# Fused softcap attention and max-out layer on one core: another order for the first eleven quads of pairs

## The chip, the core and the metric

The kernel runs on one core of a Trainium2 chip. TensorE (PE) multiplies, ScalarE (ACT) does tanh and exp, VectorE (DVE) adds, copies and normalizes, GpSimd (POOL) issues the loads, and SyncE (SP) issues the stores, the crossbar transposes and some of the signals between engines. Each engine takes its own instructions in the order in which the program has them, and waits for others by semaphores. The metric is the device time of one execution in microseconds (us), the median of the runs shown; less is better.

## What is computed

Attention with 8 batches, 12 heads, 448 positions and 64 features a head, whose scores go through a soft cap, and then a layer whose two branches are joined by a maximum:

```python
scores = (1 / 8) * q @ k.T
scores = 30 * np.tanh(scores / 30)
attn = np.exp(scores - scores.max(-1))
attn = attn / (attn.sum(-1) + 1e-9)
out = attn @ v                      # (8, 12, 448, 64)
x = out.transpose(0, 2, 1, 3).reshape(3584, 768)
g = np.maximum(x @ w1, x @ w2)      # (3584, 1024)
result = g @ w_out                  # (3584, 768)
```

Inputs and output are float32. The kernel works in bfloat16 with float32 sums. It uses max(a, b) = b + relu(a - b): it subtracts w2 from w1 once (`wd_sb`), multiplies w2 and w_out once (`wm_sb`), and computes x @ wm + relu(x @ wd) @ w_out.

## The kernel before

**Tiles.** Two heads make a pair i (0 to 47) and two pairs a quad t (0 to 23); six pairs are a batch. Scores are computed transposed, with the keys on the partitions: three blocks of 128 keys for each pair (j = 0 to 2) and the 64 left-over keys of a whole quad together. There are two score tiles in PSUM, s0 and s1, of two banks each, and four single banks, 0 to 3, for everything else. A score tile is written by S or L, read by a tanh, and lent once a quad to the value products (VL, V), until the normalization (N) has read it.

**The order.** The whole program is a list, `ORDER`, written out by hand: a semicolon between steps, each a name and numbers. The loop at the end runs it step by step (lines 737 to 740), and each step issues its instructions to its engine. So the list fixes the order on every engine, and nothing is rescheduled. Where a step stands relative to steps of other engines matters only for which data it finds and which buffers are free. The steps:

| step | engine | what it does |
|---|---|---|
| ld0, cd, Xh, XCh | SP/ACT, ACT/DVE, PE, DVE | load, cast, transpose and copy the first pair |
| lq, lk, lv, lw1, lw2, lwo | POOL | load q, k, v, and parts of w1, w2, w_out (casting) |
| D bank n | PE | n blocks of 128 columns of warming products, four to an instruction (`keep_warm`, line 466); their result is not used |
| X i bank, XC i | PE, DVE | transpose q and k of pair i (line 453), copy to `qkT` (458) |
| W c bank, WC c | PE, DVE | transpose part c of w2 (411), copy (415) |
| OP, P c h n, PC c h | PE, DVE | n of the eight premultiplies for part c, half h of `wm_sb` (426), copy (432) |
| S i j, T i j, E i j0 j1 | PE, ACT, ACT | scores (509), tanh (514), exp (531) of pair i |
| L t, TL t, EL t | PE, ACT, ACT | the same for the left-over keys (523, 527, 534) |
| VL t, V t u j0 j1 | PE | value products of quad t (595, 601), half u |
| A, B | DVE | sums of exponentials over key blocks, from quad 3 on (543, 548) |
| Y t bank, Y1 to Y3, N t u | PE, DVE | sum over keys (561, 565, 568), inverse (573 to 579), normalize into `xT` (613, 616) |
| sub c | DVE | a piece of w1 - w2 (397) |
| O g bank, M x y n | PE | open group g; n steps of groups x and y (640) |
| ev g, eva g | DVE, ACT | evict a finished group (661 for `gT`, 697 or 695 for the output rows) |
| Hs g, H g | SP, DVE | hand group g's bank over (649) |
| cr t, st b t | SP | crossbar transpose of quad t, from quad 5 on (470); store rows (671 to 676) |

**Groups and hand-overs.** A group is one bank's accumulation of the layer: stage 1 (448 columns, x @ wd) or stage 2 (384 columns, the output). A step M x y does one product of group x on rows 0 to 63 of the array and one of group y on rows 64 to 127, side by side. Each group goes through both halves, one after the other. When it changes its half, `Group.step` lets the new half's product wait for an empty instruction that `hand_over` had put on SP (Hs) or DVE (H), and which itself waits for the last product of the old half. If the list has no hand-over for a change of halves, there is no such wait. As SP and DVE take their instructions in order, a hand-over runs only when what is ahead of it on that engine has run.

**What sets the order around the change.** Quads 0 to 4 are transposed by TensorE (X, XC) and quads from 5 on by the crossbar on SP's queue (cr); there are two `qkT` buffers and two `kqs` buffers that the loads fill. The first quads also carry the setup of the weights (W, P, sub). From about quad 6 on each quad repeats a similar pattern.

Of the kernel before, what the change touches and what calls it, by code (L numbers as in the profile page):

```python
# [9 lines left out]
ld0 q; ld0 q 1; cd q; ld0 k; ld0 k 1; ms; dm; ms0; cd k; id; lq 2 0; lk 3 0; lq 3 0; lk 2 0; lw2 3; lw2 2; D 3 24;  # L10
Xh 0 0 0; Xh 0 1; cd k 1 1; cd q 1 1; XCh 0 1; XCh 0 0; D 3 4; X 1 1; S 0 0; S 0 1; XC 1; T 0 0; T 0 1; D 0 5; D 1 8;
# [8 lines left out]
X 5 0; P 2 1 4; P 0 0 3; P 2 1 1; XC 5; PC 1 1; PC 0 0; T 3 2; T 4 0; E 3 2 3; OP 3 1 3; P 3 1 1; P 2 1 1; S 4 1;  # L20
S 4 2; Y 1 1; T 4 1; T 4 2; L 2; P 3 1 4; VL 1; TL 2; V 1 1 0 3; V 1 0 0 3; S 5 0; X 6 0; E 4 0 3; T 5 0; EL 2; Y1 1;
Y2 1; PC 2 1; Y3 1; N 1 1; N 1 0; XC 6; X 7 2; W 4 1; S 5 2; S 5 1; X 8 0; P 3 1 3; WC 4; XC 8; PC 3 1; T 5 1; T 5 2;
OP 4 0 1; P 4 0 2; OP 0 1 0; P 0 1 3; S 6 0; S 6 1; W 5 3; P 0 1 1; P 4 0 6; P 0 1 4; E 5 0 2; T 6 1; T 6 0; E 5 2 3;
XC 7; sub 2 0; WC 5; sub 4 0; PC 4 0; sub 0 0; PC 0 1; OP 5 1 3; P 5 1 4; S 6 2; L 3; Y 2 1; T 6 2; TL 3; E 6 0 3;
# [36 lines left out]
M 25 24 1; S 17 1; lk 22 1; M 25 24 2; ev 22; M 25 24 1; T 17 1; S 17 2; lq 22 0; M 25 24 1; ev 23; M 25 24 1;
# [139 lines left out]
def kernel(  # L201
# [17 lines left out]
    B, H, S, D = q.shape  # L219
# [554 lines left out]
```

## Time and profile before

| | us |
|---|---|
| median of 3 runs | 328.32 |
| lowest and highest | 327.58, 328.42 |
| the profiled execution | 328.19 |
| its span, first to last instruction | 326.4 |
| TensorE busy | 319.9 |
| ScalarE busy | 281.0 |
| VectorE busy | 240.2 |
| GpSimd busy | 161.8 |

The profile is one execution. A row of a timeline gives start, duration, engine, line, operation, the tiles written and read, shape and count; in brackets stand the idle time ahead of it and what ended that. Rows of one line that follow each other are merged. "Idle" and "busy" of TensorE come from modelled ends of pipelined matmuls, so distances between starts say more than busy time. The queue of an engine that issues a DMA has rows of its own (SPq, POOLq), whose duration is that of issuing; the landing comes later.

### The profile page before, as it was taken

Reading aid. Unit: us, or ns where it says so; the run is one execution under the profiler, and the core shown is the slowest. Engines: PE = TensorE matmul, PEld = TensorE weight load, DVE = VectorE, ACT = ScalarE, POOL = GpSimd, SP = SyncE. Lnnn points to the kernel's source line nnn. Section 1 sums busy time; section 2 is a strip of 40 time slices with the busy share of each in tenths; the row PEclk is TensorE's granted clock in tenths of the full one; section 3 lists DMA queues with packets and bytes.
Section 4 is the critical chain, followed back from the end, with each engine's and each line's share of the span. In section 5 each row is a group of like instructions: output and inputs, shape, how many; then the busy total and the mean of one; then the engine's idle time right before and its main releaser. Section 6 shows DMA issues by size and latency. Waiting matters only on the chain.

```text
span 326.4 us, 9772 instructions
## 1 busy us (share of the span) xinstructions
PE 319.9 (98%) x4138; PEld 183.6 (56%) x4138; DVE 240.2 (74%) x422; ACT 281.0 (86%) x278; POOL 161.8 (50%) x237
## 2 busy tenths in 40 slices
PE   7999999999999999999999999999999999999994
PEld 3454545545656664565565565556466555557662
DVE  3346899987897778987897788968878779773201
ACT  5999999999999999999999999999999999921120
POOL 7357583677764682665775475578538311000000
PEclk9999999999999999999999999999999999999999
DMA  8999999899999999999999999999999963013033
GB/s 181 180 201 178 273 252 115 95 141 140 189 183 109 142 189 184 97 89 181 167 181 113 202 106 189 121 166 163 184 109 90 212 157 44 2 50 98 0 98 96
DMA packets 134507, 46.28 MB, mean 142 GB/s; under 512 B 112320, under 2 KB 129472, under 8 KB 134464
## 3 DMA queue, kind: packets, MB, share of 16 engines
q0 software_dynamic: 94592, 25.02, 77.6%
q1 hardware_dynamic: 39424, 19.99, 29.9%
q8 instruction: 32, 0.52, 0.7%
q10 hardware_dynamic: 448, 0.66, 0.6%
q14 instruction: 11, 0.09, 0.1%
HBM read 47.78 MB, written 11.01 MB: 180 GB/s over the span
## 4 chain that ended last, share of the span: by engine, by line
PE 94%; DMA 2%; DVE 1%; POOL 1%; issue 0%
PE mm L640 61%; PE s L509 9%; PE s L601 9%; PE mm L426 5%; DMA w2b<-in_moe_w_dram 2%; PE s L523 2%; PE mm L568 2%; PE s L595 2%; PE mm L635 1%; POOL kqs L316 1%; PE mm L453 1%; PE mm L411 1%; PE mm L561 1%; DVE xT L616 0%; PE mm L466 0%; DVE xT L613 0%
## 5 line engine op out<-in xcount | busy, mean ns | idle before, releaser
L514 ACT ACTIVATE e<-s 128x896 bf16<-128x896 f32 x144 | 125.7, 926 | 5.5 <-PE s L509 5.0
L531 ACT ACTIVATE e<-e 128x1792 bf16<-128x1792 bf16 (+2 forms) x72 | 122.8, 1708 | 0.0
L640 PE MATMUL mm<-wo_sb,gT 64*128 64x384 bf16 x864 | 115.2, 323 | 0.0
L640 PE MATMUL mm<-wm_sb,xT 64*128 64x384 bf16 x648 | 102.1, 322 | 0.0
L640 PE MATMUL mm<-xT,wd_sb 64*128 64x448 bf16 x768 | 97.6, 349 | 0.0
L323 POOL DMA_DIRECT2D kqs<-in_k_dram x76 | 54.6, 720 | 55.1 <-DMA qkT<-kqs 50.9
L640 PEld LDWEIGHTS <-gT 64*128 64x128 bf16 x864 | 58.6, 94 | 25.6 <-issue 1.1
L640 PEld LDWEIGHTS <-wd_sb 64*128 64x128 bf16 x768 | 48.3, 94 | 27.1 <-issue 2.1
L640 PEld LDWEIGHTS <-xT 64*128 64x128 bf16 x648 | 50.1, 94 | 18.5 <-issue 0.2
L509 PE MATMUL s<-qkT 64*128 64x448 bf16 x288 | 52.5, 352 | 0.2 <-DVE xT L613 0.2
L347 POOL DMA_DIRECT2D vp<-in_v_dram x48 | 30.4, 637 | 37.4 <-PE s L509 25.4
L661 DVE TENSOR_SCALAR gT<-mm 128x448 bf16<-128x448 f32 x64 | 39.0, 618 | 8.4 <-PE mm L640 7.6
L323 POOL DMA_DIRECT2D kqs<-in_q_dram x38 | 35.0, 922 | 3.9 <-issue 1.8
L601 PE MATMUL s<-e,vp 128*32 128x448 bf16 x576 | 36.1, 354 | 0.0
L543 DVE TENSOR_TENSOR esum<-e 128x896 bf16<-128x896 bf16 x42 | 25.9, 618 | 9.1 <-ACT e L531 9.1
L616 DVE TENSOR_TENSOR xT<-s,inv 64x448 bf16<-64x448 f32 x48 | 29.8, 622 | 1.7 <-PE s L601 0.8
L543 DVE TENSOR_TENSOR esum<-esum,e 128x896 bf16<-128x896 bf16 x42 | 26.2, 624 | 5.9 <-ACT e L531 4.8
L509 PEld LDWEIGHTS <-qkT 64*128 64x128 bf16 x288 | 18.7, 94 | 20.1 <-issue 11.3
L695 ACT COPY osb<-mm 128x384 f32<-128x384 f32 x10 | 4.8, 479 | 26.9 <-PE mm L640 26.7
L697 DVE COPY osb<-mm 128x384 f32<-128x384 f32 x44 | 23.3, 554 | 6.2 <-PE mm L640 5.7
L548 DVE TENSOR_TENSOR esum<-esum,el 64x896 bf16<-64x896 bf16 x42 | 26.0, 619 | 1.2
L573 DVE STREAM_TRANSPOSE st<-mm 128x448 f32<-128x448 f32 x24 | 15.6, 649 | 12.9 <-PE mm L568 11.3
(57 smaller groups left out, 269.9 us busy)
## 6 DMA issues: line engine op xcount, KB each, us to landing
out_dram<-osb SPq DMA_DIRECT2D x54, 192.0 KB, 4.8
vp<-in_v_dram POOLq DMA_DIRECT2D x38, 160.0 KB, 3.9
kqs<-in_q_dram POOLq DMA_DIRECT2D x46, 112.0 KB, 5.3
kqs<-in_k_dram POOLq DMA_DIRECT2D x76, 56.0 KB, 3.9
osb<-in_moe_w_dram POOLq DMA_DIRECT2D x4, 512.0 KB, 6.9
w2b<-in_moe_w_dram POOLq DMA_DIRECT2D x6, 256.0 KB, 7.7
wo_sb<-in_moe_w_out_dram POOLq DMA_DIRECT2D x4, 384.0 KB, 9.9
vp<-in_v_dram POOLq DMA_DIRECT2D x10, 128.0 KB, 7.8
```

What stands on the lines that cost most here:

```text
L323: nc.gpsimd.dma_start(out=to, in_=x)
L347: nc.gpsimd.dma_start(out=to, in_=x)
L509: scored[i, j] = nc.tensor.matmul(s[:, h, :S], k_of(t, o, h, j), q_of(t, o, h)).ins
L514: nc.scalar.activation(expo[i][:, 2 * j : 2 * j + 2, :], slots[i, j][:, :, :S], AF.Tanh, scale=scale / cap)
L531: nc.scalar.activation(e, e, AF.Exp, scale=float(cap))
L543: nc.vector.tensor_add(d, e[:, 0:2, :] if j == 1 else d, e[:, 2 * j : 2 * j + 2, :])
L548: nc.vector.tensor_add(d, d, left_e[t][r, :, :])
L601: nc.tensor.matmul(vals[t][place(m, u), u, :S], w[:, m, :], expo[2 * t + o][:, 2 * j + h, :], start=False, stop=(j == NJ - 1))
L616: nc.vector.tensor_mul(x[64 - r : 128 - r], vals[t][r : r + 64, u, :S], sums[t, 3][64 - r : 128 - r])
L640: ins = nc.tensor.matmul(self.ps, w[r], x[r], start=first, stop=self.at == [self.n, self.n]).ins
L661: nc.vector.tensor_relu(gT[b // 2][:, f, cs], ps)
L697: nc.vector.tensor_copy(o[:, hs], ps)
```

## The change

The list `ORDER` is written anew up to the products of quad 10 (about the first 140 us of the span). On POOL the order is the same, load by load. On the other engines the same steps stand in another order up to quad 10, with these differences in kind: banks of many steps (W, OP, X, Y, O) change; groups 24, 26 and 29 are evicted by ScalarE (eva) instead of VectorE (ev); groups 1, 10, 12, 17, 24 and 27 get a hand-over at a change of halves where there was none, group 40 gets its second one from SP instead of DVE, and several others change between SP and DVE. Warming products are as many as before (96 blocks); six of them stand between W 3 and W 2 and others move within the first pairs. From S 23 0 on each engine's order is the old one, except for the hand-overs of group 40; the text of the list differs there as well, since steps of different engines stand otherwise among each other. The instructions of TensorE are the same in number and kind over the whole program.

In `transposes`, the condition for taking a new bank asks whether a bank is named; for the steps in both lists the outcome is the same.

The diff, cut:

```diff
-ld0 q; ld0 q 1; cd q; ld0 k; ld0 k 1; ms; dm; ms0; cd k; id; lq 2 0; lk 3 0; lq 3 0; lk 2 0; lw2 3; lw2 2; D 3 24;
...
-D 3 1; D 1 4; S 0 2; D 1 4; L 0; D 1 16; T 0 2; TL 0; E 0 0 3; D 1 12; S 1 2; S 1 0; X 3 3; X 2 0; W 3 2; W 2 1;
-T 1 0; T 1 2; lw2 1; lwo 0 0; lwo 0 1; lw2 0; lq 4 0; lk 4 0; lv 0 0; lv 0 1; XC 3; XC 2; WC 3; D 0 4; S 1 1; D 0 8;
-D 2 2; S 2 1; W 1 2; WC 2; WC 1; T 1 1; T 2 1; S 2 0; D 0 4; L 1; OP 3 0 0; P 3 0 2; OP 1 0 1; P 1 0 4; P 3 0 2;
-OP 2 0 3; P 2 0 7; P 1 0 1; P 2 0 1; P 1 0 1; P 3 0 2; P 1 0 2; PC 2 0; PC 1 0; E 1 2 3; E 1 0 2; TL 1; T 2 0; EL 0;
-S 3 0; S 2 2; P 3 0 1; W 0 2; P 3 0 1; X 4 3; T 2 2; T 3 0; VL 0; Y 0 1; V 0 0 0 3; V 0 1 0 3; S 3 1; lwo 1 0;
...
-st 0 1; M 16 14 1; Hs 15; T 14 1; cr 8; B 6 0; M 16 15 1; S 14 2; M 16 15 1; ev 14; M 16 15 1; T 14 2; O 17 2;
-M 17 15 2; H 16; M 17 15 1; B 6 1; M 17 16 2; E 13 2 3; M 17 16 1; ev 15; O 18 3; M 18 16 1; L 7; VL 6; A 6 1 2;
...
-O 26 3; M 26 24 1; T 17 2; M 26 24 1; A 8 0 1; Hs 25; S 18 0; M 26 24 1; lk 23 0; M 26 25 1; A 8 0 2; M 26 25 1;
-Hs 24 2; E 17 0 2; M 26 25 1; S 18 1; lk 23 1; M 24 25 1; Hs 26; M 24 25 4; lq 23 0; M 24 25 3; T 18 0; O 27 0;
-M 27 25 1; A 8 1 1; M 27 25 1; cr 10; M 27 25 1; M 27 26 1; ev 24; M 27 26 1; T 18 1; M 27 26 1; S 18 2; ev 25;
...
+lv 0 1; E 0 0 3; lwo 1 0; S 1 2; S 1 0; X 3 3; lwo 1 1; X 2 0; XC 3; lq 5 0; W 3 2; XC 2; T 1 0; D 3 2; lk 5 0;
+D 1 4; W 2 3; WC 3; T 1 2; lv 1 0; S 1 1; WC 2; D 2 4; lv 1 1; T 1 1; S 2 1; D 0 8; T 2 1; S 2 0; W 1 0; T 2 0; L 1;
+WC 1; TL 1; S 2 2; OP 2 0 3; P 2 0 2; T 2 2; P 2 0 1; OP 3 0 0; P 3 0 1; OP 1 0 2; P 1 0 2; P 3 0 1; E 1 2 3;
+P 3 0 2; S 3 0; P 1 0 1; EL 0; P 3 0 2; P 1 0 1; P 2 0 1; P 3 0 1; T 3 0; P 3 0 1; P 2 0 1; P 1 0 1; PC 3 0; P 1 0 1;
+P 2 0 1; E 1 0 2; P 1 0 2; P 2 0 1; W 0 1; PC 1 0; S 3 1; WC 0; X 4 0; T 3 1; Y 0 2; XC 4; lk 8 0; EL 1; lq 8 0;
...
+M 15 14 1; T 14 0; S 14 1; A 6 1 1; O 16 1; M 16 14 1; Hs 15; st 0 1; lq 18 0; M 16 14 2; M 16 15 1; T 14 1; B 6 1;
+M 16 15 1; S 14 2; lk 19 0; M 16 15 1; A 6 0 2; O 17 2; M 17 15 1; T 14 2; M 17 15 1; Hs 16; cr 8; M 17 15 1; B 6 0;
+lk 19 1; M 17 16 2; E 13 2 3; L 7; ev 15; lq 19 0; VL 6; V 6 0 0 2; TL 7; A 6 1 2; V 6 1 0 2; V 6 0 2 3; ev 14;
+st 0 2; E 14 0 3; V 6 1 2 3; Y 6 0; lv 8 0; M 17 16 1; Hs 17; Y1 6; O 18 3; M 18 16 1; S 15 0; M 18 16 1; lv 8 1;
...
+Hs 25; cr 10; M 26 24 1; Hs 24; M 26 25 1; E 17 2 3; lk 23 0; M 26 25 2; M 24 25 2; lk 23 1; S 18 1; E 17 0 2;
+M 24 25 3; lq 23 0; S 18 2; M 24 25 2; Hs 26; M 24 25 1; st 1 3; O 27 0; M 27 25 2; T 18 1; M 27 25 1; A 8 1 1;
+M 27 26 4; T 18 2; A 8 1 2; M 27 26 4; B 8 1; eva 24; L 9; VL 8; ev 25; TL 9; V 8 1 0 2; B 8 0; V 8 1 2 3; st 1 4;
...
-        if c != 1:
+        if bank is not None:
             turned["qk", i] = mm_tile(bank).bitcast(bf16)
```

More of the change, by code (lines that the diff above doesn't have):

```diff
@@ L20 @@
[L20 to L24, printed above, removed]
@@ L195 @@
[L195 to L196 removed]
+ld0 q; ld0 q 1; ld0 k; ld0 k 1; ms; dm; ms0; D 3 24; id; lq 2 0; lk 3 0; lq 3 0; lk 2 0; cd k; cd q; Xh 0 0 0; lw2 3;
+Xh 0 1; cd k 1 1; D 3 4; lw2 2; XCh 0 1; cd q 1 1; XCh 0 0; lw2 1; X 1 1; lwo 0 0; S 0 0; XC 1; S 0 1; T 0 0; D 0 5;
+lwo 0 1; D 1 8; T 0 1; D 3 1; lw2 0; D 1 4; S 0 2; lq 4 0; D 1 4; T 0 2; L 0; lk 4 0; D 1 16; TL 0; lv 0 0; D 1 12;
@@ new lines @@
+M 8 9 1; Y3 4; EL 5; M 8 9 1; Hs 10; M 8 9 1; S 11 1; M 8 9 1; N 4 0; M 8 9 1; T 11 1; M 8 9 3; N 4 1; O 11 0;
+M 11 9 3; E 11 0 2; M 11 10 5; ev 9; M 11 10 1; S 11 2; M 11 10 1; ev 8; M 11 10 2; T 11 2; lq 16 0; M 11 10 1;
+A 5 1 1; S 12 0; M 11 10 1; O 12 2; M 12 10 1; T 12 0; M 12 10 1; H 11; A 5 0 2; M 12 10 1; lv 6 3; S 12 1;
+M 12 11 1; Hs 10; cr 7; B 5 1; M 12 11 1; T 12 1; lv 6 0; M 12 11 1; M 10 11 1; S 12 2; B 5 0; M 10 11 1; lk 16 1;
+M 10 11 1; T 12 2; M 10 11 4; lk 17 0; M 10 11 1; E 11 2 3; O 13 1; M 13 11 1; ev 10; L 6; st 0 0; lk 16 0; VL 5;
@@ new lines @@
+T 29 1; lv 15 2; M 55 54 1; ev 52; S 29 2; M 55 54 1; ev 53; M 55 54 1; lv 15 3; O 56 3; M 56 54 1; T 29 2;
+M 56 54 1; Hs 55; A 14 0 1; S 30 0; M 56 54 1; lk 34 1; M 56 55 2; E 29 0 2; A 14 0 2; Hs 54; M 56 55 1; S 30 1;
+lq 34 0; M 54 55 1; Hs 56; cr 16; M 54 55 5; lk 35 0; M 54 55 2; T 30 0; O 57 1; M 57 55 1; A 14 1 1; M 57 55 1;
+lk 35 1; M 57 55 1; M 57 56 1; ev 54; T 30 1; M 57 56 2; S 30 2; st 3 3; lq 35 0; ev 55; M 57 56 2; T 30 2;
+M 57 56 1; B 14 0; M 57 56 4; B 14 1; E 29 2 3; M 57 56 1; st 3 4; O 58 2; M 58 56 2; L 15; VL 14; A 14 1 2; TL 15;
@@ new lines @@
+V 14 0 0 2; V 14 1 0 2; E 30 0 3; Y 14 0; V 14 0 2 3; V 14 1 2 3; Y1 14; S 31 0; M 58 56 1; M 58 57 1; Y2 14;
+M 58 57 1; Hs 56; M 58 57 1; Y3 14; M 56 57 2; Hs 58; M 56 57 1; lk 36 0; M 56 57 1; N 14 0; M 56 57 2; T 31 0;
+M 56 57 1; lv 16 0; M 56 57 1; N 14 1; O 59 0; M 59 57 2; EL 15; M 59 57 1; lv 16 1; M 59 58 1; S 31 1; M 59 58 2;
+lv 16 2; T 31 1; M 59 58 1; ev 56; S 31 2; M 59 58 1; ev 57; M 59 58 1; lv 16 3; M 59 58 1; T 31 2; M 59 58 1;
+A 15 0 1; S 32 0; lk 36 1; M 59 58 3; E 31 0 2; A 15 0 2; O 60 3; M 60 58 1; lq 36 0; S 32 1; Hs 59; M 60 58 2;
@@ new lines @@
+M 60 59 2; Hs 58; lk 37 0; M 60 59 1; M 58 59 2; T 32 0; Hs 60; cr 17; M 58 59 1; A 15 1 1; M 58 59 1; lk 37 1;
+M 58 59 3; T 32 1; B 15 0; M 58 59 1; lq 37 0; S 32 2; O 61 1; M 61 59 1; ev 58; M 61 59 1; T 32 2; M 61 59 1;
+M 61 60 1; B 15 1; M 61 60 2; st 3 5; E 31 2 3; O 62 2; M 62 60 1; ev 59; M 62 60 2; H 61; L 16; ev 60; VL 15; TL 16;
+st 3 6; V 15 0 0 2; A 15 1 2; V 15 1 0 2; E 32 0 3; M 62 61 1; Y 15 0; V 15 0 2 3; V 15 1 2 3; Y1 15; S 33 0;
+M 62 61 2; Y2 15; O 63 3; M 63 61 1; Y3 15; M 63 61 1; Hs 62; M 63 61 1; M 63 62 1; T 33 0; M 63 62 1; N 15 0;
@@ new lines @@
+M 81 79 1; M 81 80 1; lq 44 0; M 81 80 1; ev 78; S 39 2; S 40 0; M 81 80 1; ev 79; T 39 2; O 82 3; M 82 80 1;
+lk 45 0; M 82 80 1; Hs 81; A 19 0 1; M 82 80 1; M 82 81 1; E 39 0 2; M 82 81 1; lk 45 1; ev 80; S 40 1; M 82 81 1;
+O 83 2; M 83 81 1; A 19 0 2; M 83 81 1; lq 45 0; Hs 82; cr 21; M 83 81 1; M 83 82 2; ev 81; M 83 82 1; T 40 0;
+M 83 82 2; A 19 1 1; M 83 82 3; T 40 1; M 83 82 1; B 19 0; S 40 2; M 83 82 2; T 40 2; O 84 0; M 84 82 1; B 19 1;
+M 84 82 2; H 83; H 82; E 39 2 3; M 84 83 3; M 82 83 1; L 20; A 19 1 2; VL 19; TL 20; V 19 0 0 2; V 19 1 0 2;
@@ new lines @@
+E 40 0 3; Y 19 1; V 19 0 2 3; V 19 1 2 3; Y1 19; lk 46 0; S 41 0; M 82 83 2; Y2 19; lv 21 0; M 82 83 2; Y3 19;
+M 82 83 2; lv 21 1; M 82 83 1; O 85 1; M 85 83 1; N 19 0; M 85 83 2; T 41 0; lv 21 2; M 85 84 2; N 19 1; M 85 84 2;
+lv 21 3; EL 20; M 85 84 2; S 41 1; M 85 84 1; lk 46 1; M 85 84 1; T 41 1; M 85 84 1; ev 82; S 41 2; M 85 84 1;
+lq 46 0; ev 83; M 85 84 1; O 86 3; M 86 84 1; T 41 2; M 86 84 1; Hs 85; A 20 0 1; S 42 0; M 86 84 1; M 86 85 1;
+lk 47 0; M 86 85 1; E 41 0 2; A 20 0 2; Hs 84; M 86 85 1; S 42 1; M 84 85 1; Hs 86; lk 47 1; cr 22; M 84 85 4;
@@ new lines @@
+lq 47 0; M 84 85 3; T 42 0; O 87 2; M 87 85 1; A 20 1 1; M 87 85 2; M 87 86 1; ev 84; T 42 1; M 87 86 2; S 42 2;
+st 5 3; ev 85; M 87 86 2; T 42 2; M 87 86 1; B 20 0; M 87 86 4; B 20 1; E 41 2 3; M 87 86 1; st 5 4; O 88 0;
+M 88 86 2; L 21; VL 20; A 20 1 2; TL 21; V 20 0 0 2; V 20 1 0 2; E 42 0 3; Y 20 1; V 20 0 2 3; V 20 1 2 3; Y1 20;
+S 43 0; lv 22 0; M 88 86 1; M 88 87 1; Y2 20; M 88 87 1; Hs 86; M 88 87 1; Y3 20; lv 22 1; M 86 87 2; Hs 88;
+M 86 87 2; N 20 0; lv 22 2; M 86 87 2; T 43 0; M 86 87 2; N 20 1; lv 22 3; O 89 1; M 89 87 2; EL 21; M 89 87 1;
@@ new lines @@
+M 89 88 1; S 43 1; M 89 88 2; T 43 1; M 89 88 1; ev 86; S 43 2; M 89 88 1; ev 87; M 89 88 2; T 43 2; M 89 88 1;
+A 21 0 1; S 44 0; M 89 88 3; E 43 0 2; A 21 0 2; O 90 3; M 90 88 1; S 44 1; Hs 89; M 90 88 2; M 90 89 2; Hs 88;
+M 90 89 1; M 88 89 2; T 44 0; Hs 90; cr 23; M 88 89 1; A 21 1 1; M 88 89 4; T 44 1; B 21 0; M 88 89 1; S 44 2;
+O 91 2; M 91 89 1; ev 88; M 91 89 1; T 44 2; M 91 89 1; M 91 90 1; B 21 1; M 91 90 2; st 5 5; E 43 2 3; O 92 0;
+M 92 90 1; ev 89; M 92 90 2; H 91; L 22; ev 90; VL 21; TL 22; st 5 6; V 21 0 0 2; A 21 1 2; V 21 1 0 2; E 44 0 3;
@@ new lines @@
+M 104 102 2; Hs 103; M 104 102 1; M 104 103 2; Hs 102; M 104 103 1; M 102 103 2; Hs 104; st 6 1; M 102 103 6;
+O 105 0; M 105 103 2; eva 102; M 105 103 1; M 105 104 2; eva 103; M 105 104 1; O 106 1; M 106 104 2; Hs 105;
+M 106 104 1; M 106 105 2; ev 104; M 106 105 1; O 107 2; M 107 105 2; Hs 106; M 107 105 1; M 107 106 2; ev 105;
+M 107 106 1; O 108 3; M 108 106 2; Hs 107; st 6 2; M 108 106 1; M 108 107 2; ev 106; M 108 107 1; O 109 0;
+M 109 107 2; H 108; M 109 107 1; M 109 108 2; ev 107; M 109 108 1; O 110 1; M 110 108 2; Hs 109; M 110 108 1;
@@ new lines @@
+M 110 109 2; ev 108; M 110 109 1; O 111 2; M 111 109 2; Hs 110; M 111 109 1; M 111 110 2; ev 109; M 111 110 1;
+O 112 3; M 112 110 2; Hs 111; M 112 110 1; M 112 111 2; ev 110; M 112 111 1; O 113 0; M 113 111 2; Hs 112;
+M 113 111 1; M 113 112 2; ev 111; M 113 112 9; O 114 1; M 114 112 2; Hs 113; M 114 112 1; M 114 113 2; Hs 112;
+M 114 113 1; M 112 113 2; Hs 114; M 112 113 6; O 115 2; M 115 113 2; eva 112; M 115 113 1; M 115 114 2; eva 113;
+M 115 114 3; st 7 3; M 115 114 6; O 116 3; M 116 114 2; Hs 115; M 116 114 1; M 116 115 2; Hs 114; M 116 115 1;
@@ L197 @@
+M 114 115 2; Hs 116; M 114 115 6; O 117 0; M 117 115 2; eva 114; M 117 115 1; M 117 116 2; eva 115; M 117 116 3;
+st 7 4; M 117 116 6; M -1 116 2; Hs 117; M -1 116 1; M -1 117 2; Hs 116; M -1 117 1; M 116 117 8; M -1 117 2;
+eva 116; M -1 117 1; O 118 1; M 118 118 1; eva 117; M 118 118 4; st 7 5; M 118 118 9; O 119 2; M 119 119 2; ev 118;
+M 119 119 12; ev 119; st 7 6;
 """
```

292 lines of the change are left out of this document (122 added, 170 removed).

## Prediction

> **What bounds the kernel now.** I read the page first: the span, the engine totals and the chain that ended last.
>
> ```profile
> span 326.4 us, 9772 instructions
> PE 319.9 (98%) x4138; PEld 183.6 (56%) x4138; DVE 240.2 (74%) x422; ACT 281.0 (86%) x278; POOL 161.8 (50%) x237
> ...
> PE 94%; DMA 2%; DVE 1%; POOL 1%; issue 0%
> ```
>
> TensorE is busy for 98% of the span, and 94% of the chain is its own. The change rewrites the stretch from about 12 to 138 us, so I read that stretch by stages (columns: stretch, its length, then PE, PEld, DVE, ACT and POOL busy, clock, DMA share, GB/s), and then who TensorE waited for.
>
> ```profile
> 12.00:20.00 8.00, 7.59 (x78) 4.26 (x73) 3.31 (x6) 7.84 (x9) 3.48 (x6) 1.00 1.27 199
> 20.00:62.00 42.00, 41.82 (x598) 21.54 (x598) 36.33 (x61) 42.00 (x41) 25.11 (x39) 1.00 1.22 195
> 62.00:108.00 46.00, 46.00 (x602) 26.89 (x600) 39.15 (x70) 44.72 (x45) 31.73 (x45) 1.00 1.36 143
> 108.00:138.00 30.00, 30.00 (x399) 17.11 (x399) 24.93 (x44) 29.11 (x30) 17.69 (x25) 1.00 1.34 160
> ```
> ```profile
> PE mm L411 <- DMA w2b<-in_moe_w_dram: 0.4, 1, 0.4
> PE s L509 <- DVE xT L613: 0.2, 1, 0.2
> ```
>
> The granted clock is 1.00 throughout. Two engines are full: TensorE everywhere, ScalarE from 20 to 62 us. The waits list shows 0.6 us of TensorE waits in the stretch, but a matmul's end is modelled, so a short wait can hide behind a "busy" one. I therefore count by starts.
>
> **The ledger.** The rows below (TensorE's timeline: start, duration, line, operation, count) give intervals from one start to the next.
>
> ```profile
> 12.15 0.62 PE L411 MATMUL mm<-ident,w2b 128*128 128x128 bf16 x8
> 13.18 0.62 PE L411 MATMUL mm<-ident,w2b 128*128 128x128 bf16 x8 [0.41 <-DMA w2b<-in_moe_w_dram]
> ...
> 20.35 0.55 PE L509 MATMUL s<-qkT 64*128 64x448 bf16 x4
> 20.84 0.34 PE L426 MATMUL mm<-wo_sb,w2T 128*128 128x384 bf16 x1
> ...
> 23.35 1.31 PE L601 MATMUL s<-e,vp 128*32 128x448 bf16 x24
> 24.59 0.36 PE L509 MATMUL s<-qkT 64*128 64x448 bf16 x2
> ...
> 34.58 1.07 PE L453 MATMUL mm<-ident,kqs 64*64 64x64 bf16 x56
> 35.58 0.62 PE L411 MATMUL mm<-ident,w2b 128*128 128x128 bf16 x8
> 36.36 0.55 PE L509 MATMUL s<-qkT 64*128 64x448 bf16 x4 [0.16 <-DVE xT L613]
> ...
> 58.51 2.81 PE L640 MATMUL mm<-xT,wd_sb 64*128 64x448 bf16 x28
> 61.16 0.35 PE L509 MATMUL s<-qkT 64*128 64x448 bf16 x2
> ...
> 138.63 0.36 PE L509 MATMUL s<-qkT 64*128 64x448 bf16 x2
> ```
>
> Fourteen pairs of 448 columns take 61.16 - 58.51 = 2.65, or 0.189 each; by columns a 384-wide pair or single is 0.163. Two score pairs take 20.84 - 20.35 = 0.49, which is two of 0.189 and 0.1 for the change of the array's mode; six groups of four value products in 24.59 - 23.35 = 1.24 leave the same 0.1. From the first W at 12.15 to S 23 0 at 138.63, both orders issue the same products: 171 pairs of 448 columns in M, 181 of 384, 96 P, 64 S, 66 V groups, 6 W (0.457), 6 X (0.464), 22 L and VL (0.20), 8 short Y (0.189), 3 long Y (0.77), 18 warming blocks of 128 columns (0.053); the small kinds are read from their own rows in the same way, as two X from 34.58 to 35.58. That is 116.75 us. Both orders also change mode 73 times, 7.3 us. The work is 124.05 us in either; before it took 126.48. So 2.42 us of waits and lags is all that the reordering can remove, whatever else it does. Behind S 23 0 every engine runs its old order, and ahead of W 3 nothing changes.
>
> **What goes.** The second W started 1.03 behind the first instead of 0.457: 0.57. S 5 2 started 0.78 behind its W instead of 0.557: 0.22. The other 1.63 is spread over small lags that no row names.
>
> **What stays or comes.** For the new order I walk TensorE along the ledger and ask at each S, V, Y and M whether its input is there.
>
> *A, 0.25.* The new order puts six warming blocks (0.32) between the two W, so the second could start at 12.15 + 0.457 + 0.32 = 12.93. Its weights still land where the load queue put them, just ahead of 13.18.
>
> *B, 0.42.* S 2 2 moves ahead of the premultiplies. It writes the score tile that T 2 0 reads.
>
> ```profile
> 12.48 3.73 ACT L514 ACTIVATE e<-s 128x896 bf16<-128x896 f32 x4
> ...
> 28.23 1.72 ACT L514 ACTIVATE e<-s 128x896 bf16<-128x896 f32 x2
> 29.83 0.96 ACT L531 ACTIVATE e<-e 128x896 bf16<-128x896 bf16 x1
> ```
>
> A tanh follows the one before after 0.80 and ends 0.93 behind its start. S 1 1 is at 13.18 + 0.557 = 13.74, its tanh at 14.14 (the product takes 0.36), T 2 1 at 14.94, T 2 0 at 15.74, over at 16.67. S 1 1, four warming blocks, S 2 1, eight blocks, S 2 0, W 1 and L 1 take 2.56 on the ledger, so S 2 2 is due at 16.30 and waits. In return ScalarE's pause among those four tanhs (3.73 against 3 x 0.80 + 0.93) shrinks, and it runs 0.5 ahead up to 47 us. The places where TensorE then meets it (S 3 2, Y 1, S 5 2) come out free, so the 0.22 is gone. VectorE's chain behind N 2 1 has the same work and starts about 0.6 earlier, so N 3 1 ends in time for S 9 2.
>
> *Loads, 0.* The load queue keeps its order. lk 8 waits for X 4, which the ledger puts 0.2 later.
>
> ```profile
> 22.42 0.55 POOL L316 DMA_DIRECT2D kqs<-in_k_dram x1 [0.80 <-PE mm L453]
> ...
> 24.62 0.53 POOL L316 DMA_DIRECT2D kqs<-in_q_dram x1 [1.10 <-DMA wo_sb<-in_moe_w_out_dram]
> ```
>
> The queue stops for 1.10 us two loads later for a landing that does not depend on X 4; this covers the 0.2. Without the cover, 0.2 would reach X 7.
>
> *Evictions, 0.* Groups 24, 26 and 29 are evicted by ScalarE: three of about 0.48.
>
> ```profile
> L695 ACT COPY osb<-mm 128x384 f32<-128x384 f32 x10 | 4.8, 479 | 26.9 <-PE mm L640 26.7
> ```
>
> That is 1.4 us; ScalarE's idle time in 62 to 138 us was 1.28 + 0.89 = 2.2 (the stages above). Behind them stand TL 9, T 19 1 and E 19 2, for which V 9 and S 19 wait; without that cover it is 1.4.
>
> *C, 0.3, and D, 1.25: SyncE's queue.* The crossbar transposes (cr), the stores and the hand-overs Hs share it.
>
> ```profile
> L470 SPq DMA_TRANSPOSE qkT<-kqs x19: 1301/1598/2663, 55.1 to 262.2; - x19
> ...
> DMA to landing us min/median/max: 4.2/6.3/9.5
> ```
> ```profile
> 55.50 0.75 PE L640 MATMUL mm<-xT,wd_sb 64*128 64x448 bf16 x6
> ```
> ```profile
> 55.06 1.58 SPq L470 DMA_TRANSPOSE qkT<-kqs  x1
> ```
> ```profile
> L649 SPq EVENT_SEMAPHORE  x1: 17/17/17, 56.7 to 56.7; - x1
> ```
> ```profile
> 87.02 2.19 SPq L470 DMA_TRANSPOSE qkT<-kqs  x1
> 89.27 1.26 SPq L676 DMA_DIRECT2D out_dram<-osb  x2
> ```
> ```profile
> DMA to landing us min/median/max: 7.8/7.8/7.8
> ```
> ```profile
> 95.82 0.54 PE L509 MATMUL s<-qkT 64*128 64x448 bf16 x4
> ```
> ```profile
> L649 SPq EVENT_SEMAPHORE  x3: 17/17/17, 107.6 to 108.8; - x3
> ```
> ```profile
> 109.11 1.59 SPq L470 DMA_TRANSPOSE qkT<-kqs  x1
> ```
>
> Issuing a transpose holds the queue for 1.30 to 2.66 us. The hand-over of group 3 shows that nothing passes: its products were over by about 56.1 (two of the three pairs at 55.50), yet it ran at 56.7, when the issue that began at 55.06 had ended at 56.64. There it cost nothing; group 3 went on at 58.5. The new order has, on this queue, Hs 25, cr 10, Hs 24, with only six pairs of products between the last M 25 24 and the M 24 25 that needs Hs 24. Counted from the start of that last M 25 24: it ends after 0.32, Hs 25 runs, the transpose's issue begins 0.33 later (108.8 to 109.11) and lasts 1.60, Hs 24 and TensorE's answer take about 0.1: 2.39 in all. M 24 25 is due after 0.163 + 6 x 0.163 = 1.14. TensorE stands for 1.25, from 0.95 to 2.3 with the shortest and the longest issue. Queued behind M 24 25 is everything: TensorE has one queue, and S 18 1, for which ScalarE waits, comes next. The Trainium skill (DMA: Bandwidth & Descriptors, Issuing engines are not separate DMA queues) says that starting a DMA takes an issuing sequencer a time that is usually small relative to the DMA itself. By that rule D would be about 0 and the time 327.5; this trace differs, with 1.6 of 6.3 us. C is the same thing milder: cr 8 now comes behind Hs 16, whose products end at 86.7, so its issue starts near 87.05, and the store behind it holds the queue until about 90.5. Hs 17 is needed at 90.4 (0.2 late), and S 16 0, now due at 94.6 instead of 96.0 (the second pair of the 95.82 row), meets a landing at 87.05 + 7.8 = 94.85 (the transfer begun at 87.02 has the landing row of 7.8; all nineteen took 4.2 to 9.5): 0.1, with what Hs 17 moved it. Bounds 0 and 0.5.
>
> *E, 0.8.* Lags with no name: 0 if the new order has none, 1.6 if all recur. The kinds and number of mode changes are the same, so I take half.
>
> Sum: 0.25 + 0.42 + 0.3 + 1.25 + 0.8 = 3.02, against 2.42: 0.6 longer. The profiled execution took 328.19, with 326.4 of span and 1.8 around it (median of the runs 328.32). Forecast 328.8; its own range, from the bounds of C, D and E, is 327.4 to 330.8.
>
> **Rivals.** *Nothing is held* (faster). If the transfer is handed to the queue early enough, or TensorE does not need Hs 24 so soon, D is 0; with half of E as well, 2.42 - 0.25 - 0.42 - 0.3 - 0.4 = 1.05 is won: 327.1. For it: ScalarE and VectorE meet TensorE in time everywhere I looked. Against it: the row at 56.7.
>
> *The eighth transpose lands late* (slower). S 16 0 has lost the 1.2 us that it had behind cr 8's landing (94.8 against 96.0). If that transfer takes the longest seen, 9.5 instead of 7.8, TensorE stands 1.7 more: 330.5. It decides from a landing after 95.4, and each further us is a us. Against it: the median is 6.3.
>
> *The early gain does not come* (about the same or slower). VectorE is at 36.33 of 42 us in 20 to 62; if its order makes N 1, N 3 or Y 3 late by what ScalarE gained, another 0.5: 329.3.
>
> **How the numbers follow.** Forecast 0.62, nothing held 0.14, late landing 0.20, no early gain 0.04. About 0.3%, 1 us, is what a measurement of this kernel can tell from no change: 327.3 to 329.3 around the median. The forecast's spread puts 0.03 below, 0.38 within and 0.21 above this. Faster is 0.03 + 0.14 = 0.17; same 0.38 + 0.03 = 0.41; slower 0.21 + 0.20 + 0.01 = 0.42. The range 327.2 to 330.4 leaves out most of the first rival and the end of the second.
>
> **What would show it.** A gap of about 1.2 us on TensorE in front of the first M 24 25 near 108 us, with Hs 24 directly behind a transpose's issue; the second W's wait shrunk to 0.25 and a new one of 0.4 at S 2 2; no wait at S 5 2; S 16 0 right behind cr 8's landing; S 23 0 at about 139.2 instead of 138.63. A TensorE that passes M 24 25 without a gap makes the forecast wrong, and so would a wait over 1 us that I do not name.

## The result, and the profile after

The changed kernel takes 330.12 us (median of 6 runs, 329.36 to 331.41), the kernel before 328.11 beside it (6 runs, 327.58 to 328.42). The ratio is 1.0066, 95% interval 1.0054 to 1.0078: slower, by 2.0 us. The forecast was 328.8, 0.6 longer than before, with a range of 327.2 to 330.4; the direction and the place of the largest loss were right, the size was 1.4 short. The profiled execution took 330.19, 2.00 more than that of before, and its rows carry the whole difference. All medians, ranges and ratios leave out three executions that took over 1.5% more than the fastest of their kernel (333.87 in e1, 337.30 in e2, which is its profiled one, and 334.08 in e11).

From the page of after (the span, the engine totals, the chain that ended last):

```profile
span 328.4 us, 9778 instructions
PE 320.1 (97%) x4138; PEld 183.4 (56%) x4138; DVE 238.9 (73%) x419; ACT 282.0 (86%) x281; POOL 161.8 (49%) x237
...
PE 72%; ACT 24%; issue 1%; DVE 1%; SPq 1%
```

TensorE's busy time is the same (320.1 against 319.9) and the span is 2.0 longer: the time went into standing still. TensorE's share of the chain fell from 94% to 72%: the chain now comes through SyncE's queue to a wait at 92.22, one of the two below, and ahead of it runs mostly over ScalarE. Behind 92.22 it has no piece of ScalarE, and in e3, which has no wait for SyncE's queue, TensorE's share is 95%. The waits list of after says for whom (what waited, for whom, us in total, times, longest):

```profile
PE mm L645 <- SPq L654: 1.9, 2, 1.4
PE mm L471 <- DVE warm L734: 1.8, 1, 1.8
PE s L514 <- ACT e L519: 0.4, 1, 0.4
```

The second row is the start of the kernel and stands in before too. The first is new: L654 is the hand-over, and SPq is SyncE's queue. The third is S 2 2's, which was forecast as B. (All lines are 5 further down than in before.) The same four stretches as in the prediction show where it lies, in PE's busy column (stretch, length, PE, PEld, DVE, ACT, POOL, clock, DMA share, GB/s):

```profile
12.00:20.00 8.00, 7.56 (x112) 4.40 (x105) 3.14 (x5) 8.00 (x10) 3.28 (x6) 1.00 1.27 202
20.00:62.00 42.00, 42.00 (x598) 21.65 (x598) 36.56 (x61) 41.97 (x40) 25.25 (x39) 1.00 1.17 193
62.00:108.00 46.00, 45.53 (x602) 27.13 (x600) 39.99 (x71) 45.36 (x46) 32.11 (x46) 1.00 1.41 147
108.00:138.00 30.00, 28.56 (x365) 15.97 (x362) 21.09 (x38) 27.82 (x29) 16.92 (x24) 1.00 1.19 146
```

46.00 - 45.53 = 0.47 and 30.00 - 28.56 = 1.44 are the two waits, and the clock is 1.00 throughout. Here they are, on TensorE's timeline and on SyncE's:

```profile
91.03 0.73 PE L645 MATMUL mm<-xT,wd_sb 64*128 64x448 bf16 x5
92.22 0.55 PE L645 MATMUL mm<-xT,wd_sb 64*128 64x448 bf16 x4 [0.47 <-SPq L654]
...
108.48 0.65 PE L645 MATMUL mm<-wm_sb,xT 64*128 64x384 bf16 x6
110.57 0.33 PE L645 MATMUL mm<-wo_sb,gT 64*128 64x384 bf16 x1 [1.44 <-SPq L654]
...
140.57 0.37 PE L514 MATMUL s<-qkT 64*128 64x448 bf16 x2
```
```profile
87.99 2.82 SPq L475 DMA_TRANSPOSE qkT<-kqs  x1
90.86 1.25 SPq L681 DMA_DIRECT2D out_dram<-osb  x2
...
108.52 1.94 SPq L475 DMA_TRANSPOSE qkT<-kqs  x1
```
```profile
L654 SPq EVENT_SEMAPHORE  x1: 17/17/17, 92.2 to 92.2; - x1
...
L654 SPq EVENT_SEMAPHORE  x1: 17/17/17, 110.5 to 110.5; - x1
```

cr 10's issue runs from 108.52 to 110.46, Hs 24 directly behind it at 110.50, and M 24 25 at 110.57. cr 8's issue and the two stores of st 0 2 run from 87.99 to 92.11, Hs 17 directly behind at 92.16, and M 18 17 at 92.22. Counted by starts, as in the ledger, M 24 25 comes 1.76 behind the product before it instead of 0.16, M 18 17 0.82 instead of 0.19: 1.60 + 0.63 = 2.23. S 23 0, the last point at which the two orders differ, is at 140.57 against 138.63: 1.94. So the rest of the new order was 0.3 quicker than the old one, and behind S 23 0 the distance stays.

### The profile page after: what moved, and what is told of

Read it like the earlier page. It is cut to its first block, busy times and chain, and to the rows that moved or that the text cites. A ratio compares the mean times of both kernels' runs of the same rounds, so it can differ in the third digit from the quotient of the medians.

```text
span 328.4 us, 9778 instructions
## 1 busy us (share of the span) xinstructions
PE 320.1 (97%) x4138; PEld 183.4 (56%) x4138; DVE 238.9 (73%) x419; ACT 282.0 (86%) x281; POOL 161.8 (49%) x237
## 4 chain that ended last, share of the span: by engine, by line
PE 72%; ACT 24%; issue 1%; DVE 1%; SPq 1%
PE mm L645 52%; ACT e L519 11%; ACT e L536 10%; PE s L606 6%; PE s L514 6%; ACT el L539 2%; PE s L528 2%; ACT el L532 2%; PE mm L640 1%; PE mm L573 1%; PE s L600 1%; PE mm L471 1%; PE mm L458 1%; SPq L475 0%; SPq L681 0%
## 5 line engine op out<-in xcount | busy, mean ns | idle before, releaser
L536 ACT ACTIVATE e<-e 128x2688 bf16<-128x2688 bf16 (+2 forms) x72 | 123.0, 1714 | 0.1
L606 PE MATMUL s<-e,vp 128*32 128x448 bf16 x576 | 35.1, 354 | 0.0
L700 ACT COPY osb<-mm 128x384 f32<-128x384 f32 x13 | 6.2, 480 | 26.9 <-PE mm L645 26.7
L702 DVE COPY osb<-mm 128x384 f32<-128x384 f32 x41 | 21.9, 554 | 5.3 <-PE mm L645 4.8
```

The source lines that it names most:

```text
L536: nc.scalar.activation(e, e, AF.Exp, scale=float(cap))
L606: nc.tensor.matmul(vals[t][place(m, u), u, :S], w[:, m, :], expo[2 * t + o][:, 2 * j + h, :], start=False, stop=(j == NJ - 1))
L702: nc.vector.tensor_copy(o[:, hs], ps)
```

## The experiments

Theory 1 is the prediction's: SyncE takes its queue in order, so a hand-over behind a transpose's issue or a store waits for it, and TensorE for the hand-over. The rivals say that TensorE would stand there anyway, that the transfer itself disturbs it, or that the loss is the early half's. All times are device us, as median and range; "before" is the kernel before, run beside it.

**e1: cr 10 behind Hs 24.**

```diff
-Hs 25; cr 10; M 26 24 1; Hs 24;
+Hs 25; M 26 24 1; Hs 24; cr 10;
```

> The changed kernel with one step moved: cr 10 stands behind Hs 24 on SyncE's queue and no longer ahead of it. Theory 1 (the hand-over is held by the issue ahead of it): M 24 25 follows the product before it after 0.16 and not after 1.76 us, nothing else changes, and the time falls from 330.1 by 1.60 to 328.5. Theory 2 (TensorE would stand there anyway, for the next input that is late): the wait gets another name and the time stays within 0.5 of 330.1. Theory 3 (the gain is given back, because cr 10 lands later and S 20 0 meets it): between the two, with a wait at S 20 0.

329.97 (328.32 to 333.06; before 328.22; ratio 1.006, 1.003 to 1.0089). The time alone would speak against theory 1. The trace shows otherwise: M 24 25 follows without a gap (three pairs at 108.77, the next at 109.26), but this execution (331.54) has another long gap that before and after have not.

```profile
108.77 0.65 PE L645 MATMUL mm<-wm_sb,xT 64*128 64x384 bf16 x6
109.26 0.32 PE L645 MATMUL mm<-wo_sb,gT 64*128 64x384 bf16 x1
...
143.56 0.32 PE L645 MATMUL mm<-wo_sb,gT 64*128 64x384 bf16 x1
145.80 0.36 PE L514 MATMUL s<-qkT 64*128 64x448 bf16 x2 [1.92 <-DMA qkT<-kqs]
```

S 24 0 stands for the landing of cr 12, which took 10.6 us from its issue at 135.20. Smaller losses came beside it: M 18 17 waited 0.76 where after had 0.47, a hand-over held TensorE for 0.25 at 149.88, and TensorE stopped for 0.5 in X 6 0 (last section). With e1 came something not foreseen: executions 4.7 us apart, where those of before lay within 1.1. From here on the question was also what scatters them.

**e2: st 0 2 behind Hs 17.**

```diff
-st 0 2; E 14 0 3;
+E 14 0 3;
-M 17 16 1; Hs 17; Y1 6;
+M 17 16 1; Hs 17; st 0 2; Y1 6;
```

> The changed kernel with one step moved: the store st 0 2 stands behind Hs 17 and no longer between cr 8 and Hs 17. Theory 1: Hs 17 runs when cr 8's issue ends, at 90.8 and not at 92.16; M 18 17 is due at 91.6, so its wait of 0.63 goes and the time falls from 330.1 to 329.5. Theory 2 (the time is set by something later, whatever happens here): 330.1 within 0.2, the 0.63 coming back before S 23 0. If the transpose alone were enough to hold Hs 17, a wait would stay, shorter than 0.63.

329.81 (329.31 to 330.90; before 328.22; ratio 1.0049, 1.0032 to 1.0066). Inconclusive: the expected gain of 0.6 is smaller than the scatter, and the only trace is of the execution that took 337.30.

**e3: Hs 24 on VectorE's queue.**

```diff
-Hs 25; cr 10; M 26 24 1; Hs 24;
+Hs 25; cr 10; M 26 24 1; H 24;
```

> The changed kernel with cr 10 left where it is, and group 24's hand-over given to VectorE's queue (H 24) in place of SyncE's (Hs 24). It tells the queue from the transfer. Theory 1 (the queue holds the hand-over): no gap at M 24 25, 328.5, as when cr 10 is moved. Theory 2 (the transfer itself disturbs TensorE or its inputs while it is issued at 108.5 to 110.5): the gap of 1.6 stays and the time is 330.1. VectorE's queue can hold the hand-over as well, by one of its instructions of 0.6, so up to 329.1 still speaks for theory 1.

329.23 (327.95 to 331.54; before 328.22; ratio 1.0041, 1.0022 to 1.0061). The profiled execution took 328.21, 1.98 less than that of after, and its waits list has no row for a hand-over, while the transpose is issued at full length:

```profile
108.02 2.09 SPq L475 DMA_TRANSPOSE qkT<-kqs  x1
```

So it is the queue and not the transfer. The wait at M 18 17 is missing from this execution too, although the edit does not touch it: cr 8 was held 2.19 here and 2.82 in after. The median fell by only 0.9, because slower executions remain.

**e4: before, with cr 10 ahead of Hs 24.**

```diff
-Hs 25; S 18 0;
+Hs 25; cr 10; S 18 0;
-M 27 25 1; cr 10; M 27 25 1;
+M 27 25 1; M 27 25 1;
```

> The kernel before with this one part of the change alone: cr 10 moved ahead of Hs 24 on SyncE's queue. Theory 1: Hs 25 runs at 107.61, the issue begins 0.33 later and lasts 1.6, Hs 24 and TensorE's answer come at 109.6 in place of 108.78: TensorE stands 0.85 (0.55 with the shortest issue, 1.9 with the longest) and the time rises from 328.1 to 329.0. Theory 2 (the order of the other products makes the gap): 328.1 within 0.2.

329.70 (329.07 to 330.20; before 328.22; ratio 1.0042, 1.0028 to 1.0056): this one step costs 1.5 by itself, and the waits list and SyncE's queue show it:

```profile
PE mm L640 <- SPq L649: 1.4, 1, 1.4
```
```profile
107.87 2.29 SPq L470 DMA_TRANSPOSE qkT<-kqs  x1
```

The gap is 1.56 by starts; 0.85 was expected. The same transpose was held 1.59 in before and is held 2.29 here; that is the 0.7.

**e5 and e6: the halves.** Up to the opening of group 0 (48 us) one order, behind it the other: e5 has the change's order first, e6 the order of before. The two orders have issued the same steps there, but for two additions on VectorE and one score product.

> The change's order up to the opening of group 0 at about 48 us, the order of before behind it: the early half of the change alone. Theory 1 (the loss is SyncE's queue in the later half): TensorE passes 48 us at the same time in both traces within 0.3, so 328.2, between 327.9 and 328.6, with executions within about 1 us of each other as before. Theory 2 (the early half makes the executions scatter, because an input or TensorE's own code arrives late there at 35 us): median 328.8 to 329.3 with single executions over 330.

> The order of before up to the opening of group 0, the change's order behind it: the later half of the change alone. Theory 1: both waits behind SyncE's queue stay (1.6 and 0.6), so 330.1, between 329.6 and 330.6. Theory 2 (half of the loss is the early half's): 329.2.

e5: 328.30 (327.80 to 328.79; before 328.03; ratio 1.0009, 0.9999 to 1.0018). The early half alone costs nothing and scatters nothing. e6: 330.77 (330.24 to 331.45; ratio 1.0086, 1.0070 to 1.0103), above the expected 329.6 to 330.6. It has the two waits (first row; by starts 1.76 and 0.65) and one that the seam between the two orders itself makes, 1.35 by starts (second row):

```profile
PE mm L645 <- SPq L654: 2.1, 2, 1.6
...
52.29 0.55 PE L645 MATMUL mm<-xT,wd_sb 64*128 64x448 bf16 x4 [1.18 <-DVE qkT L463]
```

Without the seam e6 would be near 329.4, which agrees with the loss lying in the later half, but its size can't be read off it.

**e7 and e8: the hand-over and four stores.** H 24 as in e3, and the stores where before had them.

```diff
-Hs 15; st 0 1; lq 18 0;
+Hs 15; lq 18 0;
-M 12 13 1; O 15 0;
+M 12 13 1; st 0 1; O 15 0;
-st 0 2; E 14 0 3;
+E 14 0 3;
-M 17 16 1; Hs 17; Y1 6;
+M 17 16 1; Hs 17; st 0 2; Y1 6;
-Hs 34; st 1 5; M 35 33 1;
+Hs 34; M 35 33 1;
-M 35 34 1; st 1 6; O 36 1;
+M 35 34 1; O 36 1;
-Y3 9; M 33 31 1; Hs 32;
+Y3 9; M 33 31 1; st 1 5; st 1 6; Hs 32;
```

> The changed kernel with group 24's hand-over on VectorE's queue, and four stores at the places in SyncE's queue that they had before: st 0 1 ahead of Hs 15, st 0 2 behind Hs 17, st 1 5 and st 1 6 right behind cr 11. Theory 1 (the stores issued just ahead of cr 8 and cr 12 are what makes these transposes land late in some executions, beside holding Hs 17): 327.9 with executions within 1 us of each other, cr 8 issued at about 87.4 and held 2.2 and not 2.8, cr 12 held about 1.6 and not 3.0. Theory 2 (the landings scatter for another reason): 329.2 as with the hand-over alone, executions scattered over 3 us.

> The order of before up to the opening of group 0, and behind it the changed order with the hand-over on VectorE's queue and the four stores moved as in e7. It puts the two halves together: if the later half without its waits is any better than before, 327.8; if theory 2 of e7 holds with the scatter in the later half, 329.2; if the scatter is the early half's, 327.8 here and 329 for e7.

e7: 327.76 (327.26 to 328.71, 12 runs; before 328.03; ratio 0.9996, 0.9984 to 1.0007). The whole loss is gone, and all twelve executions lie within 1.5. Its page and its waits list (the wait that is left is S 2 2's):

```profile
span 325.6 us, 9776 instructions
...
PE mm L471 <- DVE warm L734: 1.8, 1, 1.8
PE s L514 <- ACT e L519: 0.4, 1, 0.4
```

e8, the same behind before's early half: 328.95 (328.22 to 329.27; ratio 1.0024, 1.0014 to 1.0034). It has e6's seam (1.34 by starts), a wait of 0.30 for cr 8's landing and none of the queue waits; without the seam it would lie at 327.6, beside e7.

**e9 and e10: the stores by pairs.** H 24 with st 0 1 and st 0 2 moved alone (e9), or st 1 5 and st 1 6 alone (e10); the lines are those of e7.

> The changed kernel with group 24's hand-over on VectorE's queue and only the two stores around cr 8 moved back (st 0 1 ahead of Hs 15, st 0 2 behind Hs 17). It divides what e7 won over e3 (329.2 to 327.8, and the scatter). If it lies at cr 8: 327.8 to 328.1 here, executions within 1.5 us of each other. If it lies at cr 12, ahead of which st 1 5 and st 1 6 stand: 329, still scattered, with a wait at S 24 0 in the slower executions.

> The other half: the hand-over on VectorE's queue and only st 1 5 and st 1 6 moved back, right behind cr 11. If the stores around cr 8 are the cause: 329.2 and scattered as in e3, with waits at M 18 17 (0.3) and in some executions at S 16 0. If those ahead of cr 12 are: 328.1 (e7 and the 0.3 of Hs 17), with cr 12's issue down from some 3 us to 1.6. If both share it, 328.5 in both runs.

e9: 328.62 (327.64 to 330.07; before 328.40; ratio 1.0016, 1.0000 to 1.0031). e10: 328.85 (327.95 to 331.50; ratio 1.0023, 1.0002 to 1.0044). Neither pair alone takes the scatter away (ranges of 2.4 and 3.6, against 1.5 in e7); both together do. The medians are near the 328.5 that was expected if both pairs share the loss, but the intervals of e3, e9 and e10 overlap, so how it divides is not shown. e10, where st 0 2 still stands ahead of Hs 17, has that wait, and e9 has none there:

```profile
91.56 1.12 PE L645 MATMUL mm<-xT,wd_sb 64*128 64x448 bf16 x10 [0.39 <-SPq L654]
```
```profile
90.99 1.86 PE L645 MATMUL mm<-xT,wd_sb 64*128 64x448 bf16 x17
```

**e11: before, with the change's places for three stores.**

```diff
-st 0 1; M 16 14 1; Hs 15; T 14 1; cr 8;
+M 16 14 1; Hs 15; st 0 1; T 14 1; cr 8;
-M 31 30 3; st 1 5; E 19 2 3;
+M 31 30 3; E 19 2 3;
-M 33 31 1; st 1 6; Y3 9;
+M 33 31 1; Y3 9;
-Hs 34; M 35 33 1;
+Hs 34; st 1 5; M 35 33 1;
-T 21 2; M 35 34 1;
+T 21 2; st 1 6; M 35 34 1;
```

> The kernel before with the change's places for three stores and nothing else: st 0 1 behind Hs 15, so right ahead of cr 8; st 1 5 and st 1 6 behind Hs 34, nearer to cr 12. Theory (a store issued just ahead of a transpose delays its issue and its landing): cr 8 is issued 1.1 later, its landing meets S 16 0, cr 12 is held longer, and the time rises to between 328.6 and 329.5 with executions scattered over more than 1.5 us. Rival (stores do not matter without the rest of the change): 328.0 within 0.3.

329.38 (328.52 to 331.59; before 328.40; ratio 1.0037, 1.0020 to 1.0053): moving three stores, without any other part of the change, makes the kernel before slower by about 1.0 and scatters it. (A step st is two issues, so st 1 5 and st 1 6 are four.) In its trace Hs 35, a hand-over behind these four, comes late (first row; the change itself does not have this wait, as it gives group 35's hand-over to VectorE), and S 24 0 stands (second row) until 143.89, where two releasers coincide: cr 12's landing at 143.84, 9.3 after its issue, and a tanh's end at 143.86. Which of them decides can't be told.

```profile
132.37 0.36 PE L640 MATMUL mm<-xT,wd_sb 64*128 64x448 bf16 x1 [0.38 <-SPq L649]
143.89 0.36 PE L509 MATMUL s<-qkT 64*128 64x448 bf16 x2 [0.47 <-ACT e L514]
```

At cr 8, which was expected to land on S 16 0, this execution has no wait: it landed 4.8 after its issue.

**e12: e7 with S 2 2 later.**

```diff
-S 2 2; OP 2 0 3; P 2 0 2; T 2 2; P 2 0 1;
+OP 2 0 3; P 2 0 2; P 2 0 1; S 2 2; T 2 2;
```

> The kernel of e7 with S 2 2 three premultiplies later, so that TensorE does not stand 0.45 in front of it. If TensorE sets the pace there, 0.45 goes: 327.3, faster than before by 0.2%. If ScalarE does (its tanh of S 2 2 starts no earlier, and TensorE meets ScalarE again before 48 us), nothing is won: 327.8 within 0.2.

327.92 (327.34 to 331.59; before 328.40; ratio 0.9996, 0.9975 to 1.0016). The wait at S 2 2 is gone from the trace, and the time is as in e7: no gain that can be measured. Ten of its eleven executions lie within 0.9; the one at 331.59 shows that e7's places of the stores do not exclude scatter.

**cr 12 across the traces.** The thirteen traces (before, after and all experiments but e2) give a test that no single one gives. For cr 12, us held at its issue and us to its landing:

| st 1 5 and st 1 6 stand | held | to landing |
|---|---|---|
| right behind cr 11 (before, e4, e5, e7, e8, e10, e12) | 1.56, 1.60, 1.95, 1.68, 1.94, 1.71, 2.06 | 6.8, 6.0, 6.3, 5.3, 6.0, 5.5, 7.5 |
| behind Hs 34 (after, e1, e3, e6, e9, e11) | 3.25, 3.81, 2.85, 2.79, 2.47, 2.35 | 8.1, 10.6, 7.0, 7.4, 7.3, 9.3 |

The two groups do not overlap in the time held; in the time to landing they do (up to 7.5 in the first, from 7.0 in the second). The rows of after and of e7:

```profile
132.21 2.45 SPq L681 DMA_DIRECT2D out_dram<-osb  x4
136.37 3.25 SPq L475 DMA_TRANSPOSE qkT<-kqs  x1
```
```profile
133.58 1.68 SPq L475 DMA_TRANSPOSE qkT<-kqs  x1
```

After's cr 12 landed 0.4 ahead of S 24 0 (144.50 against 144.89), e7's 3.2 ahead. A landing as late as e1's costs 2 us, one as early as e7's nothing. That this makes the scatter is likely but not shown: of the long executions only one of e1 (331.54) was profiled. At cr 8 the same test is weaker. It was held 2.54 to 2.82 in five of the six traces with st 0 1 right ahead of it, but 2.19 in e3, and 2.19 to 2.44 in the seven without; and with the store it landed no later (4.8 to 8.2 after its issue, without it 5.7 to 8.2).

## Why the prediction was right in direction and short in size

| term | forecast | profiled execution |
|---|---|---|
| ahead of the first W | 0 | 0.58 |
| A, second W | 0.25 | 0 |
| B, S 2 2 | 0.42 | 0.44 |
| C, Hs 17 and S 16 0 | 0.30 | 0.63 |
| D, Hs 24 | 1.25 | 1.60 |
| E, small lags | 0.80 | 1.12 |
| sum, against 2.42 | 3.02 | 4.37 |

4.37 - 2.42 = 1.95: S 23 0 at 140.57. E is what is left of 4.37 when the other rows are taken out. Of the 1.35 that the forecast lacks, C, D, E and the first two rows together account for about a third of a microsecond each. The direction is D's. That the median still lies within the range is in part luck: most of its room above was left for D, and the 0.58 ahead of the first W stands in no term.

*D, right; its size failed by one factor.* "The transpose's issue begins 0.33 later (108.8 to 109.11) and lasts 1.60": it began 0.34 behind Hs 25 and lasted 1.94. The other legs of the working (0.32 to Hs 25, 0.1 from Hs 24 to the product) came out within 0.03. The row of cr 10 itself in before, 1.59, would have been no better; what a single figure hid was the spread. Cr 10 was held 1.59, 1.94, 2.09 and 2.29 in before, after, e3 and e4, and the stated bounds of 0.95 to 2.3, taken from the shortest and the longest issue, hold the 1.60. (As written, D's legs add up to 2.35 and not 2.39, and B's times give 0.37 and not 0.42; neither matters here.) e3 and e4, which take the wait away and put it in alone, confirm the step.

The Trainium skill (DMA: Bandwidth & Descriptors, Issuing engines are not separate DMA queues) has the time to initiate a DMA as usually small relative to the DMA. By that, D would have been 0 and "Nothing is held" the result. These traces disagree: after's cr 10 was held 1.94 of the 5.9 it took to land, and the wait behind it was 1.60.

*C, right place, outside its bounds (0 to 0.5).* Hs 16 ran at 87.7, not at 86.7, as TensorE was later there, and cr 8's issue took 2.82 instead of the 2.19 of before, so that the queue was free at 92.1 and not at 90.5; Hs 17 was needed at 91.6. The working kept the duration that cr 8 had in before, although the change puts the store st 0 1 right ahead of it; e3, with the same store there, had 2.19, so the store alone does not fix the length. S 16 0 was not "right behind cr 8's landing": it ran at 96.21, 1.0 behind the landing at 95.23.

*"Ahead of W 3 nothing changes", wrong for this execution.* The products just ahead were slower there. The four of S 0 0 and S 0 1 took 0.54 each in after (first row) and 0.35 in before (second row), X 1's twenty-eight 0.238 and 0.193. X 1's took 0.238 in e4 as well, with the order of before, and its first W came 0.36 later than in before; so it is scatter. A first load landed later too (third row; ScalarE, after), but e6's landed as late, and its first W came at 12.12. Why the products are slower is not shown; the granted clock is 1.00 there. The first W then came at 12.73 instead of 12.15, when the second one's weights had landed, so A's wait was 0, and S 2 0 ran when it did in before (15.66 against 15.74). Against the forecast the two rows together are 0.33 worse.

```profile
L514 PE MATMUL s<-qkT x4: 537/544/553, 6.8 to 7.1; 64*128 64x448 bf16 x4
...
L509 PE MATMUL s<-qkT x4: 349/354/360, 6.5 to 6.7; 64*128 64x448 bf16 x4
...
5.08 0.56 ACT L308 CAST kqs<-kr 128x448 bf16<-128x448 f32 x1 [0.32 <-DMA kr<-in_k_dram]
...
12.73 0.62 PE L416 MATMUL mm<-ident,w2b 128*128 128x128 bf16 x8
13.19 0.49 PE L471 MATMUL mm<-warm 128*128 128x256 bf16 x2
13.52 0.61 PE L416 MATMUL mm<-ident,w2b 128*128 128x128 bf16 x8
...
17.25 0.36 PE L514 MATMUL s<-qkT 64*128 64x448 bf16 x2 [0.36 <-ACT e L519]
```

*B, right:* S 2 2 stood 0.44 by starts (last row). *The wait at S 5 2* is gone, as foreseen. *E* lies within its bounds. *Loads and evictions* at 0: nothing in e3 or e7, which keep both, speaks against it.

*The rivals.* "Nothing is held" falls with e3 and e4. "The eighth transpose lands late" did not happen in the profiled execution: cr 8 landed 7.2 after its issue, 7.8 in before. Its 330.5 is nearer to the measured time than the forecast, by another cause. But landings did hold TensorE in other traces: at cr 8 in e8 (S 16 0 stands 0.47, right behind the landing, 8.0 after an issue that the seam had made later) and at cr 12 in e1 (2.08), a place the prediction did not look at. "The early gain does not come": the early half alone (e5) is worth 0 within 0.2%, so neither an early gain nor the rival's loss of 0.5 can be read from its time. By starts, the way from the first W to the first product of group 0 takes 35.83 in after and 35.79 in before, with one score product (0.19) more in after: no loss of 0.5 there.

*What the prediction missed as a step:* the stores. It priced them as blocks of the queue alone. That the place of the stores also goes with the length of a transpose's issue (at cr 12 in all thirteen traces, at cr 8 in most), and so with the next hand-over, was in none of its terms, and st 1 5 and st 1 6 in none of its steps.

*Left open:* why e1 scatters at least as much as e3, though both take the gap away; what holds the transposes' issue when stores are near (no run shows it); and whether e7 is any better than before. From the first W to S 23 0 its trace takes 125.81 (11.98 to 137.79) against 126.48, but by the runs 327.76 and 328.03 can't be told apart.

## What to carry to other kernels

On an in-order queue price each signal by what is ahead of it: not the instruction's own 17 ns, but the issue of the transpose or the stores before it, taken from rows, with its spread: one transpose's row of one execution is not enough. When an order is changed, list for each moved store and transpose which signals now stand behind it and how many products cover them; moving one hand-over to another queue and four stores back took after's loss of 2.0 us away (e7, 327.76 with 328.03 for before beside it) and left all other steps as they were. Compare executions as well as medians: e3's best execution (327.95) is as good as those of before, and its worst is at 331.54, so the median alone tells little of what is left to mend.

## What the hardware showed unexpectedly

The time that a transpose holds SyncE's queue is not fixed, and for cr 12 it goes with the place of the stores ahead of it: it lay between 1.56 and 2.06 us where st 1 5 and st 1 6 stand right behind cr 11, between 2.35 and 3.81 where they stand behind Hs 34 (in after they end at 134.66, 1.7 ahead of its start).

In e1 and e9 TensorE stopped for 0.5 by starts inside X 6 0, at the same product (the 52nd of 56), waiting for nothing that the profile shows:

```profile
34.25 1.00 PE L458 MATMUL mm<-ident,kqs 64*64 64x64 bf16 x51
35.59 0.25 PE L458 MATMUL mm<-ident,kqs 64*64 64x64 bf16 x5 [0.34 <-issue]
```

That is e9. In both the third transfer of the instruction queue q8 began at 33.2 or 33.3, in before at 31.0. But after began its own at 33.1 without a stop, so the late transfer alone does not explain it, and the cause stays open.
